# Rows paired 0 with 2 and 1 with 3, two residuals added by VectorE, and a new written-out order, in an SSM-convolution and FFN kernel

## Chip, core and metric

The kernel runs on one core of one Trainium2 chip. The metric is device time in microseconds of one execution; several executions are timed and the median is given.

## What is computed

Two layers are applied to `x` (1 x 2048 x 512, bf16). Each is a normalised long convolution with gating, and then a normalised SwiGLU FFN, both with a residual:

```
def _A_ref(q, k, v, shift_k, ssm_k, ssm_D):      # q is layernorm(x)
    k_shift = sum over t of k shifted by t * shift_k[:, t]     # 4 taps
    kv = k_shift * v
    y = irfft(rfft(kv, 2S) * rfft(ssm_k, 2S))[:S] + kv * ssm_D # causal convolution over S = 2048
    return q * y
def _B_ref(x, w_gate, w_up, w_down):
    return (silu(x @ w_gate) * (x @ w_up)) @ w_down            # 512 -> 1792 -> 512
x = A_q
x = x + _A_ref(layernorm(x), ...); x = x + _B_ref(layernorm(x), ...)
x = x + _A_ref(layernorm(x), ...); x = x + _B_ref(layernorm(x), ...)
```

The first three lines of `_A_ref` are shortened here. `kv` and the convolution `y` do not depend on `x`, so they are computed once for both layers.

## The kernel before

The sequence is cut into four blocks of 512 rows; inside a block, row `4p + r` lies on partition `p` as residue `r` (0 to 3), each a 128 x 512 slice. The convolution is a block transform: TensorE multiplies with cosine and sine tables (`fwd`, `inv`), VectorE does butterflies (`m`, L539, L790), products `t<-X,G` and sums `Z` between the spectra `X` of `kv` and `G` of the filter, and ScalarE moves results out of PSUM ("evictions", L418, L716).

The FFN works in units of half a block: two of the four residues, 256 rows. There are 16 units: two layers, four blocks, two halves. Which two residues form half `h` is `row(h, o)`: 0 and 1, then 2 and 3, unless `EVEN` is set. A unit goes through `prologue`: layer norm (`apply_norm`: statistics on VectorE by `bn_stats`, or on ScalarE by row sums, L827 and L833; then `ve`, the variance plus epsilon; then `rstd`, a power of -0.5 on GpSimd, L813 or L839; then, on ScalarE, `nmr`, minus mean times `rstd`, L851, and `n`, L858), the product with `y` (L885; L902 and L905 in the first unit), the residual add, a second layer norm to `z`, and a transpose to `zT`: by DMA from the SP queue (L892), in the first unit by TensorE (`ptz`, L919) with copies on VectorE (L922) and ScalarE (L924). Then `ffn`: `pf` matmuls with `w_gate` and `w_up` (L310), Silu and copy out of PSUM on ScalarE (`sg` L965, `ht` L969), `ht*sg` on VectorE (L972), and `pd` matmuls with `w_down` (L985).

A unit's residual is added in one of two ways. As a rule ScalarE copies `pd` to `dn` (L1021) and VectorE adds it to `xc` (L1024). Where `X_PE` says so, and in the last unit, an identity matmul puts the row of `xc` into PSUM ahead of the `pd` matmuls (L944) and ScalarE copies the sum out (L1014, which also yields the row sums for the next norm; L992 and L998 in the last unit). The last unit's second row is kept as two halves in two PSUM banks, so that the two output copies and DMAs can run side by side.

Every operation is recorded with the engine it runs on. `ORDER` is a written-out table, one number for each operation; sorted by it, the operations are issued to the five in-order engine queues (SP's holds the DMAs). So each engine's queue is fixed by hand, and an operation that waits holds up all behind it on its engine. Buffers are rings with a few slots: the FFN's and the first transforms' PSUM results share `pf` (4 slots), `pd` (2) and `pc` (2). The order was made with costs that the program assumes for each operation, for the power 1.2 us as a rule, 2.4 us behind ScalarE statistics:

```
PW = 1.2
PWA = 2.4
EVEN = False
X_PE = lambda l, c, h: (l, c, h) in {(0, 0, 0), (1, 3, 1)}
```

The start is one long chain with little to overlap: the filter's and `kv`'s first block (`hs`, `ev`, `vt`, by tap matrices `dg`), their products, the inverse transform into `ps`, and the first unit's prologue. `inverse_half` gives the four residues' sums to `pd` and `pf` slots; residues 0 and 2 use only the sums of `Z` halves, 1 and 3 only the differences.

Of the kernel before, what the change touches and what calls it, by code (L numbers as in the profile page):

```python
# [13 lines left out]
ACT = mybir.ActivationFunctionType  # L14
# [25 lines left out]
DGE = 'DDAP'  # L40
# [4 lines left out]
EVEN = False  # L45
# [3 lines left out]
X_PE = lambda l, c, h: (l, c, h) in {(0, 0, 0), (1, 3, 1)}  # L49
RINGS = {}  # L50
ORDER = [
# [59 lines left out]
R = 4  # L111
# [126 lines left out]
def kernel(  # L238
# [14 lines left out]
    nc = tc.nc  # L253
# [23 lines left out]
    def row(h, o):  # L277
        return h + HP * o if EVEN else HP * h + o

# [25 lines left out]
    def pe(terms, n=512):  # L305
        return terms * (n / 2400 + 0.0025)
# [980 lines left out]
```

## Time and profile before

| | |
|---|---|
| timed runs, median (lowest to highest) | 347.1 us (346.98 to 347.27), 3 runs |
| profiled execution, first to last instruction | 345.6 us, clock 0.999 |
| around the profiled span (median less span) | 1.5 us |
| TensorE busy | 337.1 us (98%) |
| VectorE busy | 283.0 us (82%), 96% up to 250 us |
| ScalarE busy | 253.6 us (73%) |
| GpSimd busy | 46.5 us (13%) |

The profiled execution's own end-to-end time is not listed beside its span, so the median stands for it. In the profile, PE is TensorE's matmuls and PEld its weight loads, DVE is VectorE, ACT is ScalarE, POOL is GpSimd, SP is the queue that issues DMAs. A matmul's end is modelled, so a busy PE is not PE at its peak. Times in the trace count from the span's start.

### The profile page before, as it was taken

The numbers are of one execution on the slowest core, as the hardware profiler recorded it, in microseconds if no ns is written. First come the engines' busy times: TensorE is split into PE (matmuls) and PEld (weight loads), VectorE is DVE, ScalarE is ACT, GpSimd is POOL, SyncE is SP. The second block draws the span as 40 slices with busy tenths as digits, with TensorE's granted clock in tenths as the row PEclk, the third lists the DMA queues.
The fourth block names the chain that finished last, engine by engine and source line by source line (L and its number), as shares of the span: only waits on it lengthen the run. The fifth ranks groups of instructions, "written<-read, shape, count | busy, mean of one in ns | idle before, by whom it ended". The sixth has DMA issues, their size and how long they took to land.

```text
span 345.6 us, 6557 instructions
## 1 busy us (share of the span) xinstructions
PE 337.1 (98%) x2580; PEld 248.8 (72%) x2612; DVE 283.0 (82%) x481; ACT 253.6 (73%) x503; POOL 46.5 (13%) x46
## 2 busy tenths in 40 slices
PE   8998999999999999999999999999999999999996
PEld 7655867858687767868587867767685868777784
DVE  7897999999999998999999999989998525526120
ACT  6889999989976657878899794569684645446361
POOL 4051111104110101111110000110401000001000
PEclk9999999999999999999999999999999999999999
DMA  7999204030111715010104102130101020101011
GB/s 282 334 306 336 51 14 63 15 93 1 32 31 29 172 40 144 13 34 2 31 3 122 32 0 62 31 93 1 32 0 34 30 32 0 32 0 21 11 47 46
DMA packets 42089, 22.96 MB, mean 66 GB/s; under 512 B 33861, under 2 KB 39882, under 8 KB 42058
## 3 DMA queue, kind: packets, MB, share of 16 engines
q1 hardware_dynamic: 41904, 22.47, 25.3%
q8 instruction: 20, 0.33, 0.4%
q14 instruction: 11, 0.09, 0.1%
q10 hardware_dynamic: 154, 0.07, 0.1%
HBM read 12.33 MB, written 2.10 MB: 42 GB/s over the span
## 4 chain that ended last, share of the span: by engine, by line
PE 92%; ACT 5%; POOL 2%; issue 1%; DVE 0%; ACTq 0%
PE pf L310 55%; PE pd L985 28%; PE ps L310 5%; POOL rstd L839 2%; PE ps L457 1%; PE wm L1253 1%; ACT H L418 1%; ACT n L858 1%; PE pt L476 1%; ACT Yk L716 1%; ACT ks L513 0%; ACT ht L969 0%; PE pt L365 0%; ACT sg L965 0%; ACT hs L486 0%
## 5 line engine op out<-in xcount | busy, mean ns | idle before, releaser
L310 PE MATMUL pf<-zT,wu_sb 128*128 128x256 bf16 x896 | 110.4, 273 | 0.9 <-ACT zT L924 0.7
L310 PE MATMUL pf<-zT,wg_sb 128*128 128x256 bf16 x896 | 110.6, 273 | 0.1
L985 PE MATMUL pd<-wd_sb,ht 128*128 128x512 bf16 (+1 forms) x442 | 100.6, 372 | 1.1
L310 PEld LDWEIGHTS <-wu_sb 128*128 128x128 bf16 x896 | 87.7, 98 | 16.6 <-issue 0.9
L310 PEld LDWEIGHTS <-wg_sb 128*128 128x128 bf16 x896 | 87.7, 98 | 15.4
L969 ACT CAST ht<-pf 128x512 bf16<-128x512 f32 x112 | 64.8, 589 | 30.7 <-PE pf L310 29.2
L965 ACT ACTIVATE sg<-pf 128x512 bf16<-128x512 f32 x112 | 65.6, 601 | 19.1 <-PE pf L310 17.2
L985 PEld LDWEIGHTS <-ht 128*128 128x128 bf16 x462 | 45.0, 98 | 45.2 <-DVE ht L972 0.9
L813 POOL TENSOR_TENSOR rstd<-ve,nhalf 128x2 f32<-128x2 f32 x24 | 27.7, 1153 | 204.5 <-DVE ve L811 204.5
L972 DVE TENSOR_TENSOR ht<-ht,sg 128x1024 bf16<-128x1024 bf16 (+1 forms) x64 | 39.0, 620 | 15.2 <-ACT ht L969 10.2
L1021 ACT CAST dn<-pd 128x512 bf16<-128x512 f32 x28 | 16.1, 590 | 24.1 <-PE pd L985 22.9
L808 DVE BATCH_NORM_STATS2 bnst<-xc 128x6 f32<-128x512 bf16 x48 | 31.7, 686 | 0.7
L1024 DVE TENSOR_TENSOR xc<-xc,dn 128x1024 bf16<-128x1024 bf16 x14 | 9.6, 686 | 18.6 <-ACT dn L1021 18.6
L839 POOL TENSOR_TENSOR rstd<-ve,nhalf 128x2 f32<-128x2 f32 x8 | 15.1, 1892 | 62.4 <-ACT ve L837 62.4
L652 DVE TENSOR_TENSOR t<-X,G 128x2048 bf16<-128x2048 bf16 x18 | 22.0, 1220 | 0.1
L656 DVE TENSOR_TENSOR t<-X,G 128x2048 bf16<-128x2048 bf16 x18 | 21.9, 1217 | 0.0
L418 ACT ACTIVATE X<-ps 128x512 bf16<-128x512 f32 x32 | 18.3, 604 | 1.8 <-PE ps L310 1.4
L885 DVE TENSOR_TENSOR n<-n,Yk 128x1024 bf16<-128x1024 bf16 x15 | 10.3, 689 | 5.8 <-ACT n L858 2.8
L664 DVE TENSOR_TENSOR t<-t,t 128x2048 bf16<-128x2048 bf16 x12 | 14.6, 1220 | 0.2
L666 DVE TENSOR_TENSOR Z<-Z,t 128x2048 bf16<-128x2048 bf16 x12 | 14.6, 1220 | 0.1
L418 ACT ACTIVATE H<-ps 128x512 bf16<-128x512 f32 x24 | 14.1, 609 | 0.7 <-PE ps L310 0.7
L310 PE MATMUL ps<-hs,fwd 128*128 128x512 bf16 x36 | 11.6, 379 | 1.1 <-ACT H L418 1.1
(108 smaller groups left out, 322.5 us busy)
## 6 DMA issues: line engine op xcount, KB each, us to landing
hn<-in_A_ssm_k_dram SPq DMA_DIRECT2D x4, 512.0 KB, 5.8
vt<-in_A_v_dram SPq DMA_DIRECT2D x4, 512.0 KB, 6.1
xc<-in_A_q_dram SPq DMA_DIRECT2D x4, 512.0 KB, 5.1
out_dram<-xc SPq DMA_DIRECT2D x15, 128.0 KB, 1.8
wg_sb<-in_B_w_gate_dram SPq DMA_DIRECT2D x1, 1792.0 KB
wu_sb<-in_B_w_up_dram SPq DMA_DIRECT2D x1, 1792.0 KB, 7.7
wd_sb<-in_B_w_down_dram SPq DMA_DIRECT2D x1, 1280.0 KB, 12.9
kn<-in_A_k_dram SPq DMA_DIRECT2D x1, 512.0 KB, 4.3
```

The lines of the kernel that those rows point to most:

```text
L310: nc.tensor.matmul(o, lhsT=lhsT, rhs=rhs, start=(n == 0), stop=(n == len(terms) - 1))
L418: add("ACT", act(D), lambda: nc.scalar.activation(out=view(), in_=ps.t[:], func=ACT.Copy, scale=scale), r=[ps], w=[(buf, keys)], conv=conv)
L652: dve(n * D, lambda t1=t1, part=part: nc.vector.tensor_mul(out=t1.t[:], in0=x.t[:, sl, 0, :], in1=g.t[:, sl, part, :]), [(x, key(slots, (0 ...
L656: dve(n * D, lambda t2=t2, part=part: nc.vector.tensor_mul(out=t2.t[:], in0=x.t[:, sl, 1, :], in1=g.t[:, sl, 1 - part, :]), [(x, key(slots ...
L808: add("DVE", 0.6, lambda st=st, i=i: nc.vector.bn_stats(out=st.t[:], in_=xs[c].t[:, i, :]), r=[(xs[c], (i,))], w=[st])
L813: add("POOL", pw, lambda: nc.gpsimd.tensor_tensor(out=rstd.t[:], in0=ve.t[:], in1=nhalf.t[:].to_broadcast((P, n)), op=ALU.pow), r=[ve, nha ...
L839: add("POOL", PWA, lambda: nc.gpsimd.tensor_tensor(out=rstd.t[:], in0=ve.t[:], in1=nhalf.t[:].to_broadcast((P, n)), op=ALU.pow), r=[ve, nh ...
L965: add("ACT", act(D), lambda ps=ps, o=o, sg=sg: nc.scalar.activation(out=sg.t[:, o:o + 2, :], in_=ps.t[:], func=ACT.Silu), r=[ps], w=[(sg, ...
L969: add("ACT", act(D), lambda ps=ps, o=o, ht=ht: nc.scalar.copy(out=ht.t[:, o:o + 2, :], in_=ps.t[:]), r=[ps], w=[(ht, (o // 2,))], due=(uni ...
L972: dve(n * W, lambda sg=sg, ht=ht: nc.vector.tensor_mul(out=ht.t[:], in0=ht.t[:], in1=sg.t[:]), [sg], [ht], due=(unit, k / pairs, 0.0, "h"))
L985: nc.tensor.matmul((pds[o] if not cs.start else pds[HP]).t[:, cs], lhsT=ht.t[:, q, o * P:(o + 1) * P], rhs=wt["d"].t[:, ft, cs], start=(ft ...
L1021: add("ACT", act(D), lambda o=o: nc.scalar.copy(out=dn.t[:, o, :], in_=pds[o].t[:]), r=[pds[o]], w=[(dn, (o,))], due=(unit, 1.0, 3.0, "h"))
```

## The change

Four edits. `EVEN` is set, so half 0 is residues 0 and 2 and half 1 residues 1 and 3 (two-row operations then work on strided pairs). `X_PE` is false for all units, so the first unit takes the usual way through `dn`. `LASTV` makes VectorE add row 0 and the first half of the second row of the last unit straight from PSUM; only the second half keeps its identity matmul and ScalarE copy. And `ORDER` is another table throughout, so that every engine's queue is changed. A copy of the taps that nothing read (`tapT`) is dropped.

```
-EVEN = False
+EVEN = True
-X_PE = lambda l, c, h: (l, c, h) in {(0, 0, 0), (1, 3, 1)}
+X_PE = lambda l, c, h: False
+LASTV = True
 ORDER = [
...
 ]
...
         xpe = X_PE(layer, c, h) or unit == LAST_UNIT
+        own = lambda o, cs: xpe and not (LASTV and unit == LAST_UNIT and not (o == HP - 1 and cs.start))
         if xpe:
             for o in range(HP):
                 i = row(h, o)
                 halves = (slice(0, D // 2), slice(D // 2, D)) if unit == LAST_UNIT and o == HP - 1 else (slice(0, D),)
-                add("PE", pe(1), lambda o=o, i=i, halves=halves: [nc.tensor.matmul(
+                halves = [cs for cs in halves if own(o, cs)]
+                if not halves:
+                    continue
+                add("PE", pe(1, sum(cs.stop - cs.start for cs in halves)), lambda o=o, i=i, halves=halves: [nc.tensor.matmul(
                     (pds[o] if not cs.start else pds[HP]).t[:, cs], lhsT=ident.t[:], rhs=x.t[:, i, cs], start=True, stop=False) for cs in halves],
...
-                                                 start=(ft == 0 and not xpe), stop=(ft == NF - 1))
+                                                 start=(ft == 0 and not own(o, cs)), stop=(ft == NF - 1))
...
-            add("ACT", act(D), lambda: nc.scalar.copy(out=x.t[:, row(h, 0), :], in_=pds[0].t[:]), r=[pds[0]], w=[(x, (row(h, 0),))],
-                due=(unit, 1.0, 3.0, "h"))
+            if LASTV:
+                add("DVE", tt1(D), lambda: nc.vector.tensor_add(out=x.t[:, row(h, 0), :], in0=x.t[:, row(h, 0), :], in1=pds[0].t[:]),
+                    r=[pds[0]], w=[(x, (row(h, 0),))], due=(unit, 1.0, 3.0, "h"))
+            else:
+                add("ACT", act(D), lambda: nc.scalar.copy(out=x.t[:, row(h, 0), :], in_=pds[0].t[:]), r=[pds[0]], w=[(x, (row(h, 0),))],
+                    due=(unit, 1.0, 3.0, "h"))
...
+                if LASTV and not half_:
+                    add(eng, 0.35, lambda cs=cs: nc.vector.tensor_add(out=x.t[:, i, cs], in0=x.t[:, i, cs], in1=pds[o].t[:, cs]),
+                        r=[pds[o], (x, (i,))], w=[(x, (R + half_,))], due=(unit, 1.0, 3.0, "h"))
...
-    add("DVE", 0.1, lambda: nc.vector.tensor_copy(out=tapT.t[:], ...), r=[pt4], w=[tapT])
+    if "W" in DGE:
+        add("DVE", 0.1, lambda: nc.vector.tensor_copy(out=tapT.t[:], ...), r=[pt4], w=[tapT])
```

Around the start, the changed queues differ as follows. On ScalarE, before: the five first X evictions, an `hs` copy, `ve`, the other `hs` copy, three X, three H evictions, then `nmr` and `n`. After: both squares, three X evictions, `ve`, two X, an `hs` copy, one X, `nmr`, the other `hs` copy, the last two X, `n`, then H. In the last unit, row 0's last `pd` matmul is followed by twelve of 256 columns.

More of the change, by code (lines that the diff above doesn't have):

```diff
@@ L943, in ffn @@
                 halves = (slice(0, D // 2), slice(D // 2, D)) if unit == LAST_UNIT and o == HP - 1 else (slice(0, D),)
-                add("PE", pe(1), lambda o=o, i=i, halves=halves: [nc.tensor.matmul(
+                halves = [cs for cs in halves if own(o, cs)]
+                if not halves:
+                    continue
+                add("PE", pe(1, sum(cs.stop - cs.start for cs in halves)), lambda o=o, i=i, halves=halves: [nc.tensor.matmul(
                     (pds[o] if not cs.start else pds[HP]).t[:, cs], lhsT=ident.t[:], rhs=x.t[:, i, cs], start=True, stop=False) for cs in halves],
-                    r=[(x, (i,)), ident], w=[pds[o]] + (pds[HP:] if len(halves) > 1 else []), due=(unit, 2 / pairs, 1.9, None))
+                    r=[(x, (i,)), ident], w=[pds[HP if cs.start else o] for cs in halves], due=(unit, 2 / pairs, 1.9, None))
         cuts = [sum(GROUPS[:n]) for n in range(len(GROUPS) + 1)]
@@ L997, in ffn @@
                 copy = nc.scalar.copy if eng == "ACT" else nc.vector.tensor_copy
-                add(eng, 0.35, lambda cs=cs, copy=copy, half_=half_: copy(out=x.t[:, i, cs], in_=pds[HP if half_ else o].t[:, cs]), r=[pds[HP if half_ else o]],
-                    w=[(x, (R + half_,))], due=(unit, 1.0, 3.0, "h"))
+                if LASTV and not half_:
+                    add(eng, 0.35, lambda cs=cs: nc.vector.tensor_add(out=x.t[:, i, cs], in0=x.t[:, i, cs], in1=pds[o].t[:, cs]),
+                        r=[pds[o], (x, (i,))], w=[(x, (R + half_,))], due=(unit, 1.0, 3.0, "h"))
+                else:
+                    add(eng, 0.35, lambda cs=cs, copy=copy, half_=half_: copy(out=x.t[:, i, cs], in_=pds[HP if half_ else o].t[:, cs]),
+                        r=[pds[HP if half_ else o]], w=[(x, (R + half_,))], due=(unit, 1.0, 3.0, "h"))
                 q, qn = (nc.scalar, "ACT") if half_ else (nc.sync, "SP")
@@ L1121 @@
     add("PE", 0.25, turn_taps, r=[tapR, ident], w=[pt4])
-    add("DVE", 0.1, lambda: nc.vector.tensor_copy(out=tapT.t[:], in_=pt4.t[:].rearrange("p j dt -> p dt j")), r=[pt4], w=[tapT])
+    if "W" in DGE:
+        add("DVE", 0.1, lambda: nc.vector.tensor_copy(out=tapT.t[:], in_=pt4.t[:].rearrange("p j dt -> p dt j")), r=[pt4], w=[tapT])
     add("DVE", 0.1, lambda: nc.vector.tensor_copy(out=tapF.t[:], in_=pt4.t[:].rearrange("p j dt -> p dt j")), r=[pt4], w=[tapF])
```

116 rows, old and new, of the table ORDER are left out of this document.

## The prediction

> **What bounds the kernel now.** I read the engine table and the waits, then the chain in order of time, then the queues around its one piece that is not TensorE. The page's shares by engine say where the end is set:
>
> ```profile
> PE 92%; ACT 5%; POOL 2%; issue 1%; DVE 0%; ACTq 0%
> ```
>
> The chain in order of time (start, length, what) shows where the 8% sits:
>
> ```profile
> 14.62 4.33 PE ps L457 x20
> ...
> 20.48 0.20 ACT ve L837
> 20.68 0.07 issue
> 20.75 5.31 POOL rstd L839
> 26.08 0.30 ACT nmr L851
> 26.41 0.81 ACT n L858
> ...
> 35.05 0.49 ACT zT L924
> 35.58 8.89 PE pf L310 x80
> ```
>
> Up to 35.58 us the chain wanders through ScalarE and GpSimd; from the first FFN matmul on it is TensorE. All five TensorE waits in the list of waits lie before 35.58 and make 3.4 us. After 35.58 the queue holds 1822 matmuls of 256 columns and 497 of 512; by the chain's pieces (x8 pf in 0.87, x4 pd in 0.86) they pace at 0.1091 and 0.2158, so 306.05 us. The last matmul ends at about 342.1, 306.5 after the start: nothing to gain there but matmuls left out. So the time is T0, the start of the first FFN matmul (35.58), plus 306.5, plus 3.5 of tail (the output copies at 342.0 to 342.6 and their DMAs), 345.6 in all. The timed runs' median, 347.1, lies 1.5 above this profiled span; I carry differences over.
>
> What sets T0? The timeline's VectorE rows (start, us, operation, idle before):
>
> ```profile
> 24.05 1.43 DVE L645 TENSOR_TENSOR Z<-t,t 128x512 bf16<-128x512 bf16 x4
> 25.50 1.29 DVE L790 TENSOR_TENSOR m<-Z 128x1024 bf16<-128x1024 bf16 x2
> 28.63 0.69 DVE L902 TENSOR_TENSOR n<-n,ps 128x512 bf16<-128x512 bf16 x1 [1.83 <-ACT n L858]
> ```
>
> VectorE has the inverse transform's input at 26.8 and stands 1.83 us for ScalarE's n, which waited for a GpSimd pow of two elements per partition. That pow's length decides this case:
>
> ```profile
> 20.75 5.30 POOL L839 TENSOR_TENSOR rstd<-ve,nhalf 128x2 f32<-128x2 f32 x1 [13.99 <-ACT ve L837]
> ...
> 246.72 3.81 POOL L839 TENSOR_TENSOR rstd<-ve,nhalf 128x2 f32<-128x2 f32 x1 [5.79 <-ACT ve L837]
> ...
> 308.43 0.69 POOL L813 TENSOR_TENSOR rstd<-ve,nhalf 128x2 f32<-128x2 f32 x1 [11.26 <-DVE ve L811]
> ```
>
> With VectorE idle the same pow takes 0.69. The long one at 246.72 ran beside this:
>
> ```profile
> 246.50 1.22 DVE L666 TENSOR_TENSOR Z<-Z,t 128x2048 bf16<-128x2048 bf16 x1
> 247.63 1.22 DVE L656 TENSOR_TENSOR t<-X,G 128x2048 bf16<-128x2048 bf16 x1
> 248.77 1.22 DVE L652 TENSOR_TENSOR t<-X,G 128x2048 bf16<-128x2048 bf16 x1
> 250.02 1.23 DVE L664 TENSOR_TENSOR t<-t,t 128x2048 bf16<-128x2048 bf16 x1
> ```
>
> It ended at 250.53, 0.55 after VectorE's third two-input operation ended (249.99), in the gap before a dependent one. Nearly every slow pow ends 0.55 after such an end; usually it gets in after one operation (0.99 to 1.60), here after three. The one at 20.75 ended at 26.05, 0.58 after the last Z of a VectorE stretch unbroken from 20.43 to 25.47. So I read 5.30 as a pow kept out until that stretch broke.
>
> **The change, part by part.** *Identity matmuls.* The last unit loses one of 512 and one of 256 columns, in gapless TensorE time: 0.2158 + 0.1091 = 0.33 us off. The first unit loses two of 512; in before they run at 31.6 and before 35.58, where TensorE waits anyway: worth 0.
>
> *Last unit's adds.* Row 0's ScalarE copy (0.59) becomes a VectorE add from PSUM; VectorE's row of that kind (n<-n,ps) is 0.69. Behind row 0's last matmul stand 12 of 256 columns, 1.31 us, and VectorE idles 3.94 before its half copy, so it is hidden; without that cover it would cost 0.1. The half copy (0.42) becomes a half add; a 512 PSUM copy and a 512 PSUM two-input operation both take 0.69, so 0. The tail stays 3.5.
>
> *First unit's residual.* Two PSUM copies with row sums become two dn copies, one VectorE add (0.69) and two row-sum passes (0.73 each): 2.15 us more on the chain to the third unit. Costed below.
>
> *Pairing 0,2 and 1,3.* Rows 0 and 2 need only the two sums m, not the differences. That could free VectorE of 1.2 us ahead of n<-n,ps, but in the changed queue all four m still stand before it: 0. Strided pairs cost nothing: H<-m as 2x512 takes 0.69, as 1024 0.69. The dropped tapT copy (0.17) precedes an idle of 0.61: 0. On SP, the larger part of w_down and the next x now go ahead of its first four tiles. SP issues the x load until 25.2 (it stood 4.64 in it), and the slower w_down row lands in 12.9, so by 38.2; the first pd matmul comes 11.1 after T0, after 44: 0, and 1 us for each us it would be later than that.
>
> *The new order at the start.* To the first X matmul, TensorE has the same work with two more H products ahead of the tap products; I get 14.5 as before (14.46). ScalarE now does the squares earlier, and ve follows three X evictions instead of five and a copy. The third X group ends on TensorE at 14.5 + 12 x 0.2158 = 17.1, its eviction starts 0.2 later (as 18.78 to 18.98 in before), so ve is at 17.8 and the pow starts at 18.1, not 20.75. VectorE is then not in an unbroken stretch: it waits for each X eviction, and the product running at 18.1 ends at 18.55 before a dependent Z. The pow should end at 19.1 to 19.7. ScalarE has the fourth and fifth X (18.65, 19.5), an hs copy (20.4) and the sixth X ahead of nmr and reaches it at 20.9, so the pow stalls nobody. Behind nmr stand the second hs copy (0.9) and the last two X evictions (0.49 each): last X at 23.2, before 23.05. VectorE then has a product, three Z, three m (0.61 + 1.08 + 1.82): 26.8 as before, but n is ready at 26.4, so n<-n,ps starts at 26.85 instead of 28.63. From there before took 6.95 to T0. Now VectorE also waits for the fourth H eviction and a ks copy on ScalarE (30.7) before z at 31.4; the transposes end at 32.6; the ScalarE copy of zT at 33.3; 16 tap matmuls (0.9) queued ahead of the first FFN matmul end at 33.55. T0 = 33.55: 2.03 earlier.
>
> *The middle.* Every chain there moves. The second unit's transposes landed at about 53.7 and were needed at 55.3; ScalarE now has 1.1 us more ahead of them: 0.5 left. The third had 73.2 against 75.3, 2.1 of slack, and loses about 2.1 by the residual: near zero. VectorE, 96% busy until 250, has 0.9 us more in all. Before lost 0.45 to such stalls; I add 0.5, between 0 and 1.2. A gain of this kind is excluded, as only 0.45 is there to win.
>
> Sum: 345.6 - 2.03 - 0.33 + 0.5 = 343.7, or 1.9 under before; the median becomes 345.2.
>
> By the Trainium skill ("SBUF — State Buffer", section "Who interferes with whom") a VectorE instruction with two SBUF inputs and a GpSimd instruction that reads SBUF exclude one another for a whole instruction. The trace's 0.55 after a VectorE end agrees; that a pow loses several boundaries in a row the page does not say.
>
> **The rivals.** *First use (slower).* The 5.30 is also the first pow of the program, and its end misses the 0.55 pattern by 0.03 where the others miss by under 0.01. If the excess of 4.6 belongs to the first use, it moves along. Against it: the first tap scaling on GpSimd (0.66) is no longer than the next three (1.89 together), and 3.81 is no first use. Then the pow lasts from 18.1 to 23.4 and ScalarE stands 2.5 us at nmr, from 20.9, with the last two X evictions behind it. Last X at 25.7 (nmr 0.33, hs 0.9, X 0.49 and 0.57); 3.6 us of product, Z and m as above: n<-n,ps at 29.3; the Y eviction that the second row needs, behind n and four H on ScalarE, at 30.4; z 3.5 later, 33.9 (in before 2.9, from 30.42 to 33.35; a statistics pass of 0.6 now stands behind that product instead of ahead); the transposes and 16 tap matmuls as above, T0 at 36.15. That is +0.57 - 0.33 + 0.5 = +0.7: median 347.8, between 347.3 and 348.5 by the middle's bounds. It decides from a pow of about 4.6 us on; below that the new order still wins.
> The Trainium skill ("GPSIMD Engine Reference", section "Instruction dispatch") says the first call of a freshly loaded kernel pays about 6 us that no row shows. That would be this rival; the trace shows a first pow of 5.30 but no such cost on GpSimd's other first operations.
>
> *The middle eats it (same).* If VectorE's near-full 36 to 250 us leaves the new order late at several units, each by the 0.5 to 1 that the second and third already lose in slack, 2 us return: 345.6 - 2.36 + 2 = 345.2, median 346.7. For: the thin slacks. Against: before's order shows that such chains can be packed with 0.45 lost.
>
> **How the numbers follow.** 0.2% (0.7 us) is about what a measurement of this kernel can tell from no change. The early start: 0.50, all of it faster, 344.5 (no stall in the middle) to 346.0. First use: 0.36, half within 0.2%, mostly slower beyond. The middle: 0.14, near 346.7, with a tail of bad stalls beyond before. Faster 0.50, same 0.20, slower 0.30. The likeliest is 345.2; its own range is 344.5 to 346.0. To leave out no more than 2 in 10 the range must take in most of the first-use case: 344.5 to 348.2.
>
> **What would show it.** Right: the first rstd pow starts near 18.1 and lasts under 2 us; n<-n,ps starts near 26.9 with no wait on n; the first pf matmul near 33.5; from there about 306 us to the last matmul; the waits list shows under 1 us of TensorE waits after it. Wrong: a first pow above 4 us and ScalarE standing at nmr with X evictions behind (first use); a T0 near 33.5 with TensorE waits on zT, ht or dn later (the middle); or a tail longer than 3.5, if the PSUM adds cost more than the copies.

## The result, and the profile after

| | before | after |
|---|---|---|
| timed runs, median (lowest to highest) | 346.69 us (344.91 to 347.27), 9 runs | 344.58 us (343.69 to 344.96), 9 runs |
| ratio after to before, 95% interval | | 0.9936 (0.9918 to 0.9954), that is -2.2 us |
| profiled execution, first to last instruction | 345.59 us | 343.15 us (its own time 344.93) |
| first X product on TensorE | 14.46 | 14.62 |
| from there to the first FFN matmul (T0) | 21.12 | 18.96 |
| from T0 to the start of the last matmul | 306.32 | 306.11 |
| from there to the end | 3.69 | 3.46 |

The kernel is faster by about what was forecast (345.2 against 347.1, -1.9). The last four rows, in us from the traces, are the ledger used below: they add up to the span. An X product is one of the matmuls (`ps<-vt,fwd`) whose results the X evictions move. The changed kernel's chain of waits, share by engine, against 92% of TensorE, 5% of ScalarE and 2% of GpSimd before:

```profile
PE 91%; ACT 4%; DVE 3%; issue 1%
```

GpSimd is gone from it. The timeline of the changed kernel around the first pow (start, us, engine, line, operation, and in brackets the idle time before it):

```profile
17.90 0.29 ACT L838 ACTIVATE ve<-sm,eps 128x2 f32<-128x2 f32 x1
...
18.27 1.04 POOL L840 TENSOR_TENSOR rstd<-ve,nhalf 128x2 f32<-128x2 f32 x1 [11.57 <-ACT ve L838]
...
18.76 0.42 DVE L646 TENSOR_TENSOR Z<-t,t 128x512 bf16<-128x512 bf16 x1
```

The first pow of the program now takes 1.04 instead of 5.30. VectorE's three products end at 18.73, the Z that needs them starts at 18.76, and the pow ends at 19.31, 0.55 after the break. VectorE's rows further on, and TensorE's first FFN matmul:

```profile
25.18 1.89 DVE L791 TENSOR_TENSOR m<-Z 128x1024 bf16<-128x1024 bf16 x3
27.00 0.68 DVE L903 TENSOR_TENSOR n<-n,ps 128x512 bf16<-128x512 bf16 x1
...
31.45 0.73 DVE L864 TENSOR_SCALAR z<-xc,mv,rstd 128x512 bf16<-128x512 bf16 x2
```

```profile
33.58 1.04 PE L311 MATMUL pf<-zT,wg_sb 128*128 128x256 bf16 x8
```

`n<-n,ps` follows the last `m` with no wait in brackets, where before stood 1.83 us. TensorE's waits in the changed kernel (what waited, for what, us in total, times, longest; the list leaves out waits under 0.15) all lie before T0:

```profile
PE wm L1267 <- DVE wz L1050: 1.0, 1, 1.0
PE ps L311 <- ACT H L419: 0.4, 1, 0.4
PE ps L311 <- DVE vt L515: 0.4, 1, 0.4
```

### The profile page after: what moved, and what is told of

It reads as the page before. It is cut to its first block, busy times and chain, and to the rows that moved or that the text cites. A ratio compares the mean times of both kernels' runs of the same rounds, so it can differ in the third digit from the quotient of the medians.

```text
span 343.2 us, 6553 instructions
## 1 busy us (share of the span) xinstructions
PE 336.4 (98%) x2579; PEld 248.6 (72%) x2610; DVE 283.4 (83%) x482; ACT 253.9 (74%) x504; POOL 35.3 (10%) x46
## 4 chain that ended last, share of the span: by engine, by line
PE 91%; ACT 4%; DVE 3%; issue 1%
PE pf L311 54%; PE pd L990 28%; PE ps L311 6%; PE ps L458 1%; ACT H L419 1%; PE wm L1267 1%; DVE bnst L809 1%; ACT hs L487 1%; PE pt L477 1%; ACT X L419 0%; ACT n L859 0%; PE pt L366 0%; DVE m L540 0%; DVE t L665 0%; DVE Z L667 0%
## 5 line engine op out<-in xcount | busy, mean ns | idle before, releaser
L990 PE MATMUL pd<-wd_sb,ht 128*128 128x512 bf16 (+1 forms) x440 | 102.4, 372 | 1.2
L974 ACT CAST ht<-pf 128x512 bf16<-128x512 f32 x112 | 64.0, 591 | 29.3 <-PE pf L311 29.1
L814 POOL TENSOR_TENSOR rstd<-ve,nhalf 128x2 f32<-128x2 f32 x24 | 23.0, 958 | 217.8 <-DVE ve L812 207.6
L1034 ACT CAST dn<-pd 128x512 bf16<-128x512 f32 x30 | 17.0, 589 | 21.0 <-PE pd L990 20.9
L419 ACT ACTIVATE X<-ps 128x512 bf16<-128x512 f32 x32 | 19.2, 611 | 4.0 <-PE ps L311 3.4
L1037 DVE TENSOR_TENSOR xc<-xc,dn 128x1024 bf16<-128x1024 bf16 x15 | 10.3, 689 | 13.4 <-ACT dn L1034 13.2
L840 POOL TENSOR_TENSOR rstd<-ve,nhalf 128x2 f32<-128x2 f32 x8 | 8.7, 1088 | 59.2 <-ACT ve L838 59.1
L604 ACT ACTIVATE kc<-kTb,tapF 128x512 bf16<-128x512 bf16 x16 | 12.1, 783 | 0.0
```

Of the source, the lines that this page charges most:

```text
L419: add("ACT", act(D), lambda: nc.scalar.activation(out=view(), in_=ps.t[:], func=ACT.Copy, scale=scale), r=[ps], w=[(buf, keys)], conv=conv)
L814: add("POOL", pw, lambda: nc.gpsimd.tensor_tensor(out=rstd.t[:], in0=ve.t[:], in1=nhalf.t[:].to_broadcast((P, n)), op=ALU.pow), r=[ve, nha ...
L974: add("ACT", act(D), lambda ps=ps, o=o, ht=ht: nc.scalar.copy(out=ht.t[:, o:o + 2, :], in_=ps.t[:]), r=[ps], w=[(ht, (o // 2,))], due=(uni ...
L990: nc.tensor.matmul((pds[o] if not cs.start else pds[HP]).t[:, cs], lhsT=ht.t[:, q, o * P:(o + 1) * P], rhs=wt["d"].t[:, ft, cs], start=(ft ...
L1034: add("ACT", act(D), lambda o=o: nc.scalar.copy(out=dn.t[:, o, :], in_=pds[o].t[:]), r=[pds[o]], w=[(dn, (o,))], due=(unit, 1.0, 3.0, "h"))
```

## The experiments

The theory: the pow of 5.30 us was kept out by an unbroken stretch of VectorE operations with two SBUF inputs, and moving `ve` ahead of that stretch is most of the gain. The rivals: the pow is long for a reason of its own (first use, or that moment of the program); the identity matmuls, the pairing or the rest of the new order carry the gain. A drain is a point at which VectorE has finished one operation before it starts the next; elsewhere the next starts about 0.08 us before the last one's end. An order entry that moves is shown as a move in its engine's queue.

### `ve` alone, in the kernel before

```
 ScalarE:  X, X evictions; last pass of squares (L833)
+          ve (L837)
           X, X, X evictions; hs
-          ve (L837)
           hs; X, X, X; H, H, H; nmr; n
```

> The kernel before with one entry of its order moved: on ScalarE, ve of the first unit stands right behind the second row-sum pass (at about 17.6 us) instead of behind five X evictions and an hs copy (20.36); nothing else moves. Lock theory (the pow is kept out until VectorE's stretch of two-input operations breaks): the pow starts at about 18.0, VectorE waits there for X evictions, so the pow lasts 0.7 to 1.6; nmr is reached behind the three H evictions at about 24.5 and waits for nothing; n<-n,ps starts at 26.9 when VectorE's m are done instead of 28.63, and the first FFN matmul at 33.8 to 34.2 instead of 35.58. Time -1.2 to -1.8 us, ratio 0.995 to 0.997. Rival (the pow is long for a reason of its own at that place of the program, whatever VectorE does): the pow lasts about 5 from 18.0 to 23.3; the time falls too, as nmr is reached later than that, so the pow's length and not the time tells the two apart.

Measured: ratio to before 0.9965 (0.9954 to 0.9977), -1.2 us. GpSimd's row and VectorE's rows in its timeline:

```profile
17.58 0.72 POOL L839 TENSOR_TENSOR rstd<-ve,nhalf 128x2 f32<-128x2 f32 x1 [10.82 <-ACT ve L837]
```

```profile
25.30 1.29 DVE L790 TENSOR_TENSOR m<-Z 128x1024 bf16<-128x1024 bf16 x2
26.75 0.69 DVE L902 TENSOR_TENSOR n<-n,ps 128x512 bf16<-128x512 bf16 x1
```

The first pow of the program takes 0.72, so neither first use nor its place costs 4.6. T0 came at 33.71, but this execution's first X product was at 13.88; counted from there T0 is at 19.83 against 21.12, -1.29, which agrees with the timed runs. From T0 to the last matmul it has 306.32, exactly before's.

### A drain in the stretch, in the kernel before

```
 VectorE:  m, m (L790); product t1, product t2 of slot 2
+          Z, Z of slot 2 (L645)
           product t2 of slot 3
-          Z, Z of slot 2
           Z, Z of slot 3
```

> The kernel before with two entries moved on VectorE alone: the two Z operations of slot 2 (they need the two products just before them) stand right behind these products instead of behind one more product, so VectorE drains once at about 23.45 us in the stretch that was unbroken from 20.43 to 25.47. ve and the pow stay where they were (pow from 20.75). Lock theory: the pow gets in at that drain and ends at about 24.0 to 24.1, so it lasts 3.3 instead of 5.3; nmr is reached behind the H evictions at about 24.5 and does not wait; n<-n,ps starts at about 26.9 instead of 28.63, the first FFN matmul at 33.8 to 34.2; time -1.2 to -1.8 us. Rival (first use, or the DMA traffic of those microseconds): the pow still lasts about 5.3, the time is within 0.2 us of before.

Measured: ratio 0.9957 (0.9942 to 0.9971), -1.5 us. Its timeline, shifted by the early start of this execution (first X product at 13.74):

```profile
20.04 3.35 POOL L839 TENSOR_TENSOR rstd<-ve,nhalf 128x2 f32<-128x2 f32 x1 [13.29 <-ACT ve L837]
20.32 1.29 DVE L790 TENSOR_TENSOR m<-Z 128x1024 bf16<-128x1024 bf16 x2
...
21.52 1.29 DVE L641 TENSOR_TENSOR t<-X,G 128x1024 bf16<-128x1024 bf16 x2
...
22.84 0.76 DVE L645 TENSOR_TENSOR Z<-t,t 128x512 bf16<-128x512 bf16 x2
```

The products end at 22.81, Z starts at 22.84 because it needs them, and the pow ends at 23.39, 0.58 after the break. `ve`, the pow's place and ScalarE's queue are those of before; only the break moved, and the pow's end moved with it, so that it lasted 3.35 us, as expected. That shows the cause of the 5.30: the unbroken stretch kept the pow out.

### `ve` late, in the kernel after

```
 ScalarE:  X, X, X evictions
-          ve
           X, X; hs; X
+          ve
-          nmr
           hs; X, X
+          nmr
           n
```

> The kernel after with two entries moved on ScalarE: ve stands behind three more X evictions and an hs copy (at about 21.0 us instead of 17.9), so that the pow starts at about 21.4, inside VectorE's unbroken stretch from 19.1 to 25.15; the first nmr, which would wait for it, stands right ahead of its n instead of ahead of an hs copy and two X evictions. Lock theory: the pow lasts about 4.3, to 25.7; ScalarE stands about 2.6 us at nmr with the H evictions behind, n of row 0 is ready at about 29.2, n<-n,ps starts at 29.3 instead of 27.0, the first FFN matmul at 35.5 to 36.2 instead of 33.58; time +1.9 to +2.6 us over after, about that of before. Rival (what made the pow long in before was not VectorE's stretch): the pow lasts 1 to 1.6, nmr does not wait, and the time is that of after within 0.3.

Measured: ratio to before 0.996 (0.9943 to 0.9976). Neither expectation held:

```profile
20.32 2.12 POOL L840 TENSOR_TENSOR rstd<-ve,nhalf 128x2 f32<-128x2 f32 x1 [13.53 <-ACT ve L838]
```

```profile
22.47 0.29 ACT L852 ACTIVATE nmr<-nm,rstd 128x1 f32<-128x1 f32 x1 [0.28 <-POOL rstd L840]
```

The pow lost two boundaries between VectorE operations and then got in behind a Z that ended at 21.86, though the next product had started at 21.78, with no drain. ScalarE waited only 0.28 for it. From the first X product T0 is at 19.63, 0.67 later than after's. So a drain is not the only thing that lets the pow in.

### `ve` from VectorE, in the kernel before

```
-            add("ACT", TINY, lambda: nc.scalar.activation(out=ve.t[:], in_=sm.t[:, n:2 * n], func=ACT.Identity, scale=1.0 / D, bias=eps.t[:]),
+            add("DVE", 0.08, lambda: nc.vector.tensor_scalar(out=ve.t[:], in0=sm.t[:, n:2 * n], scalar1=1.0 / D, scalar2=LN_EPS,
+                                                             op0=ALU.mult, op1=ALU.add), ...     # first unit only
 VectorE:  m (L790); ve; m
```

> The kernel before with ve of the first unit computed by VectorE (a 128x2 operation between the two m operations, at about 21.6 us) instead of ScalarE (20.36); the rest of the order stands. In the traces so far a pow whose ve came from VectorE got in at the first boundary between overlapping VectorE operations in 50 of 55 cases, one whose ve came from ScalarE in 27 of 66. If the place of the pow's start within the VectorE operation decides: the pow starts at about 21.8 and gets in behind the second m or the next product, so it lasts 0.7 to 1.6 and ends by 23.4, n<-n,ps starts at about 26.9 and the first FFN matmul at 33.8 to 34.4, ratio 0.995 to 0.997. Rival (only a drain of VectorE lets the pow in there): it ends at about 26.1 again, the ratio is 0.999 to 1.001.

Measured: ratio 0.999 (0.997 to 1.0009). The pow started at 21.93 and lasted 4.23, to 26.16; it lost seven overlapped boundaries and got in at the drain at 25.58. T0 is at 21.18 from the first X product, within 0.06 of before's. So `ve` from VectorE does not by itself let the pow in; the rival held.

In all twelve traces together, a waiting pow got in at each of 127 boundaries where VectorE had drained (the next operation starts after the last one's end), and at 140 of 221 where the operations overlapped. What decides at the overlapped ones was not found.

### The last unit's adds alone, in the kernel before

```
+LASTV = True
 X_PE, EVEN and ORDER as before (the entries of the dropped identity matmul and of tapT taken out)
```

> The kernel before, its order and pairing, with the last unit's residual adds on VectorE alone (one identity matmul of 512 and one of 256 columns fewer there; the unused copy of the taps is left out too). By the prediction's terms: 0.33 us of TensorE off between the first FFN matmul and the last matmul (306.33 from start to start before, 306.00 expected), the first FFN matmul unchanged at 35.6, tail unchanged at 3.5 to 3.7: time -0.33, ratio 0.999. Rival (the adds from PSUM cost on the end): the tail grows by 0.1 to 0.3 and the time stays.

Measured: ratio 0.9983 (0.9971 to 0.9996), -0.6 us. From T0 to the last matmul 306.00, 0.32 less than before; T0 21.13 from the first X product, unchanged; its tail 3.29. The tails of the kernels with the old end were 3.29 to 3.85, with the new end 3.28 to 3.46: the adds from PSUM cost nothing that can be seen there.

### Both small edits

> The kernel before with two small edits together: ve of the first unit early in ScalarE's queue (as in the run with ve early) and the last unit's residual adds on VectorE. If the two gains are separate they add: first FFN matmul at 33.7 to 34.2, 306.00 from there to the start of the last matmul, ratio 0.9965 x 0.9983 = 0.9948, or -1.8 us. Against the changed kernel's 0.9936 this leaves 0.1% (0.4 us) to the rest of its order, which fills a gap of 0.88 us that the order before has on TensorE ahead of the first FFN matmul with 16 tap matmuls. Rival (the new table as a whole matters, the two edits alone do not carry it): ratio above 0.997.

Measured: 344.88 us, ratio 0.9935 (0.9915 to 0.9956): the gains add within the interval, and these two edits alone (`ve` early, `LASTV`) give as much as the changed kernel in the timed runs. (The product of the two single ratios is 0.9948, inside the interval.) In the ledger it is 19.82 from the first X product to T0 (after 18.96) and 305.99 from there (after 306.11), so after's profile is still ahead by 0.7 there, less than the timed runs can tell.

### The pairing alone, twice

The first kernel has `EVEN = True` and the places of rows 1 and 2 exchanged only where the inverse product has to come first (first and last block).

> The kernel before with the pairing alone: rows 0 and 2 in the first half, 1 and 3 in the second, and in the order the places of rows 1 and 2 exchanged where their inverse products and Y evictions have to come first (first block and last block). The prediction's term is 0: the first pow still lasts 5.3, n<-n,ps still starts at about 28.6, the first FFN matmul at 35.6, ratio 0.999 to 1.001. Rival (the pairing itself saves VectorE the differences ahead of the first unit, or strided pairs cost): a shift of the first FFN matmul by 0.6 or more to either side.

Measured: ratio 1.0041 (1.0021 to 1.0061), slower, which was not expected. T0 was before's (21.12), but from T0 to the last matmul it took 307.66. One row in VectorE's timeline tells where:

```profile
92.91 0.69 DVE L885 TENSOR_TENSOR n<-n,Yk 128x1024 bf16<-128x1024 bf16 x1 [2.05 <-ACT Yk L690]
```

Half 0 of the second block now needs row 2 of `Yk`, and VectorE waits for an eviction that the old order leaves to 92.25, the last of that block's four. (Half 0 of the second block is the fifth unit, not the third, as the expectation for the second kernel calls it.) Counted from the first X product, VectorE was 2.14 us late from there on, until at 106.2 TensorE lost 1.35 us, of which the list of waits counts 1.2 as idle. Three lines of its TensorE waits, the first of them this one, and then those of the second kernel, in which the exchange was made in all four blocks; its list has no such line:

```profile
PE pf L310 <- ACT sg L965: 1.2, 1, 1.2
PE wm L1253 <- DVE wz L1037: 1.0, 1, 1.0
PE pf L310 <- ACT zT L924: 0.7, 1, 0.7
```

```profile
PE wm L1253 <- DVE wz L1037: 1.0, 1, 1.0
PE pf L310 <- ACT zT L924: 0.7, 1, 0.7
```

> The pairing alone again, now with the places of rows 1 and 2 exchanged in the inverse products and Y evictions of all four blocks. In the first run of the pairing VectorE stood 2.05 us at n<-n,Yk of the third unit (90.9 us) for an eviction of row 2 that the old order made late, and TensorE lost 1.35 us at 106. If that was only the order left unmatched in the second block: no such wait, the first FFN matmul at 35.3 to 35.6, 306.3 from there to the start of the last matmul, ratio 0.999 to 1.001 (the prediction's term 0 for the pairing). If the pairing itself costs: TensorE waits remain behind the first FFN matmul and the ratio stays above 1.002.

Measured: ratio 0.9996 (0.9983 to 1.0009), T0 21.12 from the first X product, 306.33 from there; the wait for `sg` is gone. The pairing itself is worth nothing that these runs can tell; it only needs an order that fits it.

### What the rest of the order is worth

```
 TensorE (kernel after):
-          16 tap matmuls (L311, ps<-dg,kTb)
           8 pf matmuls
+          16 tap matmuls
```

> The kernel after with one entry moved: the 16 tap matmuls that stand ahead of the first FFN matmul on TensorE go behind the first eight FFN matmuls. The first FFN matmul then waits for the zT copy: 33.45 instead of 33.58, with TensorE idle for about 0.75 from 32.7, and the 0.9 of taps comes on top later. If the total is TensorE's work plus its gaps: +0.75 us over after, ratio to before about 0.9958 instead of 0.9936. Rival (the chain to zT sets the end, TensorE's order ahead of it costs nothing): within 0.2 us of after.

Measured: ratio 0.9944 (0.9926 to 0.9961); the difference from after's 0.9936 is too small for the timed runs. In the trace TensorE loses 0.76 before T0 by the pace of its matmuls' starts (0.6 of it idle in the list of waits), T0 is at 18.84 from the first X product (0.12 earlier), and from T0 to the last matmul it takes 307.05 (0.94 more): 0.8 us worse, as expected. An earlier T0 that is bought with work put off is no gain.

The last kernel goes after TensorE's two gaps that are left in after, ahead of T0:

```
 ScalarE:  H before (nmr, n of row 2, nmr of row 0);  n of row 2 behind n of row 0;  ks before the fourth of four H
 TensorE:  two inverse products of row 1 before the X product that waits for vt
```

> The kernel after with TensorE's two remaining gaps ahead of the first FFN matmul attacked: on ScalarE the first H eviction goes ahead of the first nmr and n, and one ks eviction ahead of the last of four H evictions; on TensorE two inverse products that are ready go ahead of an X product that waits for vt. After has gaps of 0.56 us at 23.7 and 0.52 us at 30.7. If each gap closed is time won: the first FFN matmul 0.2 to 0.6 us earlier (counted from the first X product: 18.96 in after), ratio 0.992 to 0.9935. Rival (the chain m, n<-n,ps, z, zT on VectorE sets it, closed gaps reopen ahead of it): within 0.1 us of after's 18.96, ratio 0.9936.

Measured: 344.53 us, ratio 0.9942 (0.9924 to 0.996), T0 at 19.00 from the first X product: after's within 0.04. Its TensorE waits:

```profile
PE wm L1267 <- DVE wz L1050: 1.0, 1, 1.0
PE ps L797 <- DVE m L791: 0.5, 1, 0.5
PE ptz L920 <- DVE z L864: 0.3, 1, 0.3
```

The gaps at `H` and `vt` closed and opened again at `m` and `z`, two operations of VectorE: before T0 VectorE's chain is the bound now. No version of the study beats the changed kernel beyond what a measurement can tell.

## Where the prediction was right, and the step that failed

*What bounds the kernel.* Right: from T0 to the last matmul all the traces take 305.9 to 306.3, but for the unmatched pairing (1.35 lost) and the late taps (0.9 of work put there).

*The pow.* Right in its place and price: 18.27 against a forecast 18.1, 1.04 against 1.0 to 1.6, no wait at `nmr` (21.01 against 20.9), `n<-n,ps` at 27.00 (26.85), `z` at 31.45 (31.4), T0 at 33.58 (33.55). The drain shows that the stretch made it long. The first-use rival, given 0.36, fell: the first pow took 1.04 in the changed kernel and 0.72 with `ve` moved alone. The Trainium skill ("GPSIMD Engine Reference", section "Instruction dispatch") says that the first call of a freshly loaded kernel pays about 6 us; no such cost is in these rows, nor between `ve`, which ends at 18.19, and the pow at 18.27. The Trainium skill ("SBUF — State Buffer", section "Who interferes with whom") also says that a VectorE instruction with two SBUF inputs contends with a GpSimd instruction that reads SBUF, for ports that are an exclusive lock. The rows agree in one direction, with the 0.55 to 0.58 after a break; that a pow loses up to nine boundaries in a row comes on top. The other direction does not show: the two `m` behind the break at 25.47 in before take their usual 1.29, though the pow runs beside them to 26.05.

*How the 2.03 is made up.* In the changed kernel the pieces came close to the forecast: counted from the first X product, `n<-n,ps` came forward from 14.17 to 12.38, by 1.79 (1.78 forecast), and T0 behind it by another 0.37 (0.25), 2.16 in all. But the pow alone is not worth 1.78, although the prediction read the whole 1.83 of VectorE's wait as its doing. With `ve` moved alone `n<-n,ps` stood at 12.87, so the pow gives 1.30. With the old order the last `m` ends 0.38 later when `ve` goes early, and `n<-n,ps` starts 0.15 after it (26.60 and 26.75 there), not right behind it: one `m` stands between row 0's last `m` and `n<-n,ps`, and row 0's inverse products take longer than that; in the changed queue two do. The rest, 0.87 of T0, is the new order: 0.49 ahead of `n<-n,ps`, 0.28 between it and `z`, 0.10 from `z` to T0. So moving `ve` pays in full only together with an order that fits it, which the sum had in it without saying so.

*Identity matmuls.* Right: 0.33 forecast, 0.32 measured alone in the last unit (306.32 to 306.00). The first unit's way through `dn` was not run by itself.

*Adds, pairing.* Right at 0, the pairing only with the order that fits it. That it forces a new place on every row-2 eviction was not seen.

*The middle.* This is the step that failed: the sum put +0.5 on TensorE behind T0, and 0.1 came, 306.11 against the 306.00 that `LASTV` leaves alone. The prediction charged added work to the slack of the second and third units, the time by which their transposes land ahead of TensorE's need, and then counted thinner slack as lost time, with no row in which TensorE would wait. The work was over-charged too: the second unit has 1.4 of slack in before and 0.9 in after, the third 1.9 and 0.3, so they lost 0.5 and 1.6, where 1.1 and 2.1 were charged, and neither came late. What is left is one late unit that the prediction did not name. Its second transpose lands 3.8 after its issue, where most take 2.4, at 132.29, and TensorE's first matmul comes 0.2 late (in the first pair of rows, 1.73 from start to start; 1.51 in the second, from the kernel with `ve` late, where this unit is in time and the whole stretch behind T0 takes 305.90):

```profile
130.70 1.67 PE L990 MATMUL pd<-wd_sb,ht 128*128 128x512 bf16 x7
132.43 1.80 PE L311 MATMUL pf<-zT,wg_sb 128*128 128x256 bf16 x15
```

```profile
130.30 1.67 PE L990 MATMUL pd<-wd_sb,ht 128*128 128x512 bf16 x7
131.81 1.91 PE L311 MATMUL pf<-zT,wg_sb 128*128 128x256 bf16 x16
```

So the rival "the middle eats it" was right that a unit can come late, and wrong on the size: 0.2, not 2. Nor does an earlier T0 by itself eat slack: with `ve` moved alone the second and third units keep before's 1.4 and 1.9, because VectorE's queue behind T0 came forward by the same 1.87.

*The sum.* The forecast span was 343.73, the measured one 343.15. Of the 0.58 the middle makes 0.38, the tail 0.23 (3.69 carried over, 3.46 found; tails of one and the same code differ by 0.2 to 0.6 among the traces), T0 0.03 the other way, as this execution's first X product came at 14.62 and not at 14.5. The timed median, 344.58, lies 0.6 under the forecast 345.2, which is partly luck: a run takes 1.78 more than its span here and not 1.5, and the profiled run is 0.35 above the median, which nearly cancel. It lies only 0.08 above the range's lower end.

*The chances.* They do not follow from their parts: half of 0.36 is 0.18 for the same time, and most of the middle's 0.14, near 346.7, lies within 0.2% of before as well, so the same time should have had more than 0.20 and a slower one less than 0.30.

## What to carry to other kernels

A GpSimd instruction of 0.7 us, such as the pow here, can last as long as VectorE runs two-input operations without a break: give it its input where VectorE waits for something, or put an operation that depends on the one before it into VectorE's stretch, and expect the GpSimd end about 0.55 us after the break. Slack behind a bottleneck moves with the queue that feeds it, so an earlier start costs no slack there, while added work on a chain does; and slack that is lost costs time only where it runs out. Compare traces from the last common event on, not from their start.

## What had not been expected of the hardware

The first X product, behind the same input loads, started between 13.46 and 14.62 us in the twelve traces, while from it to `n<-n,ps` kernels of one start agree within 0.01 (14.17 in four traces of the old start, 12.38 in three of the new one). So spans of single profiles compare to about a microsecond, the ledger up to the last matmul to a tenth or two, its tail to half a microsecond.

Which overlapped boundary a waiting pow wins stays open: in the stretch at 20 us it lost nine of nine in before, seven of seven with `ve` from VectorE, and elsewhere most were won at the first try. Three of the 85 timed executions of before took 344.8 to 345.0 us where most others took 346 to 347.5; a pow that gets in early could make that difference, but none of the three was traced, so that is not shown.
